# Moving one more batch's transposes of u from the DMA queue to TensorE, with newly searched instruction orders, in an attention and mixer kernel

## The chip, the cores and the metric

The kernel runs on one core of one Trainium2 chip. The metric is the device time in microseconds of one execution of the whole program. A ratio of two kernels is the mean time of one kernel's fast runs divided by the mean time of the other's fast runs of the same rounds, so it isn't quite the ratio of the medians that are quoted beside it. "Fast" leaves out executions more than 1.5% above the fastest of the same kernel; one run of the kernel before (300.56 us) fell out that way. Faster or slower needs 2%.

Engine names: PE is TensorE (matmul), PEld its weight loads, DVE is VectorE, ACT is ScalarE, POOL is GpSimd, SP is SyncE, which here only issues DMAs.

## The reference

Eight batches, each of 576 tokens. First comes attention with 8 heads of 64, an ALiBi bias and a causal window of 128; then a mixer on its result x (576 x 512 per batch).

```
scores = q @ k.T / 8 + slope[h] * -(distance), masked to 0 <= distance < 128
x      = softmax(scores) @ v                       # heads side by side: [576, 512]
u      = x + (relu(x.T @ w_tok1) @ w_tok2).T       # token mixing
out    = u + relu(u @ w_ch1) @ w_ch2               # channel mixing, 512 -> 1536 -> 512
```

## The kernel before: what the change and the argument touch

Every piece of work has a short name, and five hand-searched lists give the order in which the pieces are emitted. The order within the list is the order of instructions on every engine. One prime mark after a name means the next batch, two the one after it, and so on. The lists overlap batches: while batch b is in its channel mixing, batch b+1 has its attention and token mixing and batch b+2 its scores.

```python
U_DMA = (2, 3, 4, 5, 6, 7)      # batches whose u is transposed by DMA
DVE_RELU = (2, 3, 6)            # channel groups whose relu is on DVE, the others on ACT
PROLOGUE = """
J O q0 I q23 M0 FC l1 l23 W4 l0 qt G0 v2 q1 M1 v0 M3 cq0 M2 ck1 LC m1 ck0 v1 A0 cq1 A1 S00 ...
"""
SECOND = """ ... Lk''' C4 Lq''' v3''' v0''' v2''' ... U0' U2' UT' U3' U1'
S11'' X1' S00'' X0' X2' D20 D21 S21'' S10'' E0 D30 D22 E1 D31 P0'' D32 E2 X3'
"""
# ... FIRST, PERIOD (for batches 2 to 6) and LAST ...
```

The names that the text uses: q, l, qt, v load q, k, their tails and v (q0, q1, l0, l1 are plain fp32 loads on SP, which need the casts cq and ck; the rest are casting loads on POOL). J and I build the distance table and the identity matrix. A transposes q and k of batches 0 and 1 on TensorE, S makes a group of scores with its Exp (ACT) and mask multiplication (DVE), p/P is the product with v and its normalisation, k/K and u/U are the two halves of token mixing. G loads the three parts of w_ch1 (the tile WC1), H the halves of w_ch2. x/X transposes u, C is one of 12 channel groups of `u @ w_ch1` with its relu, D and E are the second channel product. T does the tail tokens of C. W is n matmuls on zeros that are only meant to keep TensorE's clock up. Lk, Lq, Zk, Zq load k and q of batches 2 to 7 and transpose them by DMA.

```python
def utrans(b, c):                                  # X
    def dma():
        nc.sync.dma_start_transpose(               # two 128-token chunks at a time
            out=utb[b % 2][:, c:c + 2]..., in_=ub[b % 2][:, c:c + 2, :]...)
    if b in U_DMA:
        return dma if c % 2 == 0 else lambda: None
    def f():
        t = M()[:, 0:256].bitcast(bf16)            # one of three PSUM banks of the mixer
        for cb in range(NCB):                      # 4 transposes by TensorE
            nc.tensor.transpose(t[:, cb * P:(cb + 1) * P],
                                ub[b % 2][:, c, cb * P:(cb + 1) * P], ident[:, :])
        cp = nc.vector.tensor_copy if c in X_DVE else nc.scalar.copy
        cp(out=utb[b % 2][:, c, :, :], in_=t...)
    return f

def ch1(b, ht):                                    # C: needs all four chunks of utb
    def f():
        t = M()
        for cb in range(NCB):
            nc.tensor.matmul(t[:, :], lhsT=WC1[:, cb, ht * P:(ht + 1) * P],
                             rhs=utb[b % 2][:, :, cb, :], start=..., stop=...)
        # ... relu on DVE or ACT
    return f

def score(b, kb, j):                               # S
    def f():
        s = S2()                                   # one of two score buffers, two banks each
        # ... matmuls into s, Exp on ACT from s to e, mask multiplication on DVE to p
    return f
```

The softmax here doesn't subtract the row's maximum and nothing guards it: scores larger than these inputs give would overflow.

## Time and profile before

| | before |
|---|---|
| time, median of 4 runs | 296.59 us (295.94 to 297.87) |
| span of the profiled run | 294.0 us |
| PE busy | 279.2 us, 95% |
| longest single wait of PE | 3.87 us, channel matmuls of batch 2 on the DMA transposes of u |

The page of the profile, parts 1 and 2: busy time of each engine, then 40 slices of the span (7.35 us each) with the busy share in tenths, the clock that TensorE was granted, and the busy share of the DMA engines.

```profile
PE 279.2 (95%) x2666; PEld 155.4 (53%) x2666; DVE 152.8 (52%) x302; ACT 135.3 (46%) x212; POOL 99.6 (34%) x128
...
PE   4889999999999869999999999999999999999995
...
PEclk9979999999999979999999999999999999999999
DMA  7999999899999999998999956995703320141013
```

PE is full except in the first slices, in slices 13 and 14 (counted from 0) and in the last. The clock has two dents, in slice 2 and slice 14. No other engine is close to full on average, so time can only come out of these few places. (The DMA engines are 90% busy or more in most of the first 23 slices.)

The waits of PE, from the same execution (who waited for what: total us, times, longest):

```profile
PE psM L471 <- DMA utb<-ub: 3.9, 1, 3.9
PE psM L227 <- ACT ks L729: 1.7, 1, 1.7
PE psM L227 <- DVE qs L729: 1.2, 1, 1.2
PE psM L227 <- DMA ks<-in_k_dram: 1.1, 2, 0.6
```

The first line is the wait in slices 13 and 14. L471 is the channel matmul, utb the transposed u. The others belong to the first microseconds. The view of windows gives the busy time of each engine in chosen stretches, then the granted clock, the share of the DMA engines (1 is one fully loaded set; over 1 means that the times of packets overlap) and GB/s:

```profile
core 0: us, PE busy (x) PEld busy (x) DVE busy (x) ACT busy (x) POOL busy (x), PEclk, DMA share, GB/s
13.00:17.00 4.00, 2.79 (x36) 1.49 (x33) 3.66 (x10) 4.00 (x7) 2.38 (x4) 1.00 2.25 163
17.00:20.60 3.60, 3.36 (x44) 2.81 (x45) 3.46 (x10) 0.99 (x3) 2.90 (x5) 0.53 1.35 199
93.00:97.00 4.00, 4.00 (x25) 1.73 (x24) 2.40 (x5) 3.31 (x4) 4.00 (x6) 1.00 2.11 185
101.00:105.40 4.40, 0.55 (x6) 0.27 (x5) 0.19 (x1) 0.58 (x1) 0.00 (x0) 1.00 1.77 152
106.00:109.00 3.00, 3.00 (x20) 1.46 (x18) 0.00 (x0) 1.06 (x2) 0.00 (x0) 0.50 1.61 253
```

Read it from the fourth row: PE is idle for most of 101 to 105.4 us. In the fifth row it is busy all the time, but at half the clock, so about half of the 3.4 us from 106 to 109.4 us is lost as well. In the third row, where the transposes were issued (93.1 us), the DMA share is 2.11. The second row shows another half-clock stretch in the prologue.

The timeline of the issuing queue and of PE shows both ends of the wait (start us, us, engine, line, what; in brackets the idle time before it and what ended it). The line between is from the view of DMA issues: the two transposes took 10.1 us from issue to landing as the median, and the later of them 10.9 us.

```profile
93.08 4.81 SPq L451 DMA_TRANSPOSE utb<-ub  x2
...
utb<-ub SPq DMA_TRANSPOSE x2, 10.1
...
105.41 3.08 PE L471 MATMUL psM<-utb,WC 128*128 128x512 bf16 x8 [3.87 <-DMA utb<-ub]
```

### The profile page before, as it was taken

How to read it: one execution, taken by the hardware profiler on the slowest of the kernel's cores; microseconds unless marked ns; L12 is line 12 of the kernel's file. 1: busy time of each engine (PE TensorE's matmuls, PEld its weight loads, DVE VectorE, ACT ScalarE, POOL GpSimd, SP SyncE). 2: the span in 40 equal slices, each digit the busy share in tenths (PEclk: the TensorE clock that was granted, in tenths of full speed). 3: DMA queues.
4: the chain of work that ended last, by engine and by line, in shares of the span. 5: the costliest groups of instructions: out<-in, count | busy, mean ns of one | idle time of the engine just before them, and what ended most of it. 6: DMA issues, size and time to landing. Idle time of an engine off the chain costs nothing.

```text
span 294.0 us, 6361 instructions
## 1 busy us (share of the span) xinstructions
PE 279.2 (95%) x2666; PEld 155.4 (53%) x2666; DVE 152.8 (52%) x302; ACT 135.3 (46%) x212; POOL 99.6 (34%) x128
## 2 busy tenths in 40 slices
PE   4889999999999869999999999999999999999995
PEld 2567546546564335654565455655565455645443
DVE  4587467557457406566467426555556626433012
ACT  6855896148525225425633554435542563203500
POOL 8786643098419501950079003930000000000000
PEclk9979999999999979999999999999999999999999
DMA  7999999899999999998999956995703320141013
GB/s 179 171 191 187 200 182 128 163 160 188 156 162 135 121 210 155 113 162 147 164 94 166 180 138 126 133 153 162 163 0 75 106 75 0 36 109 74 0 71 109
DMA packets 150748, 38.53 MB, mean 131 GB/s; under 512 B 137920, under 2 KB 146240, under 8 KB 150720
## 3 DMA queue, kind: packets, MB, share of 16 engines
q0 software_dynamic: 103152, 17.41, 78.1%
q1 hardware_dynamic: 47568, 20.72, 32.7%
q8 instruction: 21, 0.34, 0.5%
q14 instruction: 7, 0.06, 0.1%
HBM read 35.85 MB, written 9.44 MB: 154 GB/s over the span
## 4 chain that ended last, share of the span: by engine, by line
PE 83%; DMA 11%; DVE 2%; POOL 1%; ACT 1%; issue 0%; SPq 0%; POOLq 0%; ACTq 0%
PE psM L471 29%; PE psM L519 26%; DMA WC<-in_moe_w_ch_dram 5%; PE psM L429 4%; PE psM L404 4%; PE psT L486 4%; DMA utb<-ub 4%; PE psS L280 4%; PE psM L541 3%; PE psS L343 2%; DMA ks<-in_k_dram 2%; PE psS L339 2%; PE psS L371 1%; PE psM L500 1%; PE psS L284 1%; ACT pe L293 1%
## 5 line engine op out<-in xcount | busy, mean ns | idle before, releaser
L471 PE MATMUL psM<-utb,WC 128*128 128x512 bf16 x384 | 90.2, 383 | 3.9 <-DMA utb<-ub 3.9
L519 PE MATMUL psM<-WC,r 128*128 128x512 bf16 x372 | 87.0, 379 | 0.0
L293 ACT ACTIVATE pe<-psS 128x1024 bf16<-128x1024 f32 (+1 forms) x68 | 63.3, 987 | 38.0 <-PE psS L280 34.2
L477 ACT ACTIVATE r<-psM 128x512 bf16<-128x512 f32 x72 | 42.7, 607 | 55.3 <-PE psM L471 55.3
L471 PEld LDWEIGHTS <-WC 128*128 128x128 bf16 x384 | 35.5, 98 | 43.5 <-issue 6.1
L519 PEld LDWEIGHTS <-r 128*128 128x128 bf16 x372 | 34.2, 98 | 41.2 <-issue 3.8
L183 POOL DMA_DIRECT2D kn<-in_k_dram x24 | 21.1, 894 | 81.5 <-DMA kT<-kn 77.8
L299 DVE TENSOR_TENSOR pb<-pe,masks 128x1024 bf16<-128x1024 bf16 (+1 forms) x50 | 33.2, 670 | 27.4 <-ACT pe L293 27.3
L524 DVE TENSOR_TENSOR ob<-psM,ub 128x512 f32<-128x512 f32 x31 | 21.4, 689 | 24.8 <-PE psM L519 24.8
L183 POOL DMA_DIRECT2D vp<-in_v_dram x32 | 28.9, 953 | 2.3 <-DMA ks<-in_k_dram 1.6
L474 DVE TENSOR_SCALAR r<-psM 128x512 bf16<-128x512 f32 x24 | 16.6, 691 | 13.6 <-PE psM L471 12.7
L183 POOL DMA_DIRECT2D qn<-in_q_dram x24 | 21.3, 934 | 3.0 <-DMA WC<-in_moe_w_ch_dram 2.7
L303 DVE TENSOR_TENSOR pb<-pe,masks 128x512 bf16<-128x512 bf16 x16 | 6.8, 425 | 28.6 <-ACT pe L293 28.5
L431 DVE TENSOR_TENSOR ub<-psM,xb 128x512 bf16<-128x512 f32 x28 | 18.1, 686 | 5.4 <-PE psM L429 5.1
L353 DVE TENSOR_TENSOR xb<-psS,rt 128x512 bf16<-128x512 f32 x28 | 19.4, 692 | 1.0
L280 PE MATMUL psS<-qT,kT 64*128 64x256 bf16 x192 | 17.2, 280 | 1.2 <-ACT pe L293 0.7
L486 PEld LDWEIGHTS <-WC 128*128 128x128 bf16 x384 | 13.8, 100 | 3.9 <-issue 0.8
L429 PE MATMUL psM<-r,W 128*128 128x512 bf16 x56 | 15.4, 379 | 0.2 <-DVE ob L524 0.2
L343 PEld LDWEIGHTS <-pb 128*128 128x128 bf16 x224 | 13.3, 97 | 3.6 <-DVE pb L299 0.5
L343 PE MATMUL psS<-vp,pb 128*128 128x65 bf16 x224 | 15.1, 193 | 0.0
L486 PE MATMUL psT<-utt,WC 128*128 128x64 bf16 x384 | 14.3, 196 | 0.0
L489 ACT ACTIVATE r2t<-psT 128x384 bf16<-128x384 f32 x16 | 8.0, 498 | 11.8 <-PE psT L486 11.2
(119 smaller groups left out, 280.4 us busy)
## 6 DMA issues: line engine op xcount, KB each, us to landing
out_dram<-ob SPq DMA_DIRECT2D x31, 256.0 KB, 2.2
vp<-in_v_dram POOLq DMA_DIRECT2D x32, 128.0 KB, 6.6
kn<-in_k_dram POOLq DMA_DIRECT2D x24, 128.0 KB, 4.3
qn<-in_q_dram POOLq DMA_DIRECT2D x24, 128.0 KB, 5.1
WC<-in_moe_w_ch_dram POOLq DMA_DIRECT2D x3, 512.0 KB, 7.9
WC<-in_moe_w_ch_dram POOLq DMA_DIRECT2D x2, 768.0 KB, 12.3
out_dram<-ob SPq DMA_DIRECT2D x10, 128.0 KB, 2.3
qs<-in_q_dram POOLq DMA_DIRECT2D x3, 256.0 KB, 6.2
```

Of the source, the lines that this page charges most:

```text
L183: nc.gpsimd.dma_start(out=dst, in_=src[b, :, c * P:(c + 1) * P, :].rearrange("h s d -> s h d"))
L280: nc.tensor.matmul(s[:, h, a * 256:(a + 1) * 256], lhsT=kT[i][r, kb, hp, :], rhs=qT[i][r, kb:kb + 2, hp, :], start=True, stop=True)
L293: nc.scalar.activation(out=e[:, h, :], in_=s[:, h, :], func=ACT.Exp, scale=scale)
L299: nc.vector.tensor_tensor(out=p[:, :].rearrange("p (h x) -> p h x", h=2)[:, h], in0=e[:, h, :], in1=masks[:, j, h].rearrange("p h g a x -> ...
L343: nc.tensor.matmul(ov, lhsT=prob(b, qb, h, 0), rhs=vt[:, qb, h, 0:D + 1], start=first, stop=(hh == 3))
L353: nc.vector.tensor_tensor(out=xb[b % 2][:, qb, :].rearrange("p (b h d) -> p b h d", b=2, h=4), in0=ov[:, :, :, 0:D], in1=rv[:, :, :, None] ...
L429: nc.tensor.matmul(t[:, :], lhsT=W2[:, j, c * P:(c + 1) * P], rhs=r1[b % 2][:, j, :], start=(j == 0), stop=(j == 1))
L471: nc.tensor.matmul(t[:, :], lhsT=WC1[:, cb, ht * P:(ht + 1) * P], rhs=utb[b % 2][:, :, cb, :], start=(cb == 0), stop=(cb == NCB - 1))
L477: nc.scalar.activation(out=r2[b % 2][:, ht, :], in_=t[:, :], func=ACT.Relu)
L486: nc.tensor.matmul(o, lhsT=WC1[:, cb, ht * P:(ht + 1) * P], rhs=utt[(b // 2) % 2][:, cb, b % 2, :], start=(cb == 0), stop=(cb == NCB - 1))
L519: nc.tensor.matmul(t[:, :], lhsT=r2[b % 2][:, ht, c * P:(c + 1) * P], rhs=WC2[:, ht, :], start=(ht == 0), stop=(ht == NHT - 1))
L524: nc.vector.tensor_tensor(out=o[:, :], in0=t[:, :], in1=ub[b % 2][:, c, :], op=ALU.add)
```

## The change

The intent: TensorE transposes u of batches 0 to 2, DMA the others; some score groups of batch 0 in the banks of the mixer; all order lists searched anew. The diff, cut to its core:

```diff
-U_DMA = (2, 3, 4, 5, 6, 7)
-U_ACT = (1,)
-X_DVE = (1, 2, 3)
+U_DMA = (3, 4, 5, 6, 7)
+U_ACT = (0,)
+X_DVE = (1, 3)
 PROLOGUE = """
-J O q0 I q23 M0 FC l1 l23 W4 l0 qt G0 v2 q1 M1 v0 M3 cq0 M2 ck1 LC m1 ck0 v1 A0 cq1 A1 S00 v4 A2
-v3 S20 AT S10 A3 m0 LW S30 S01 q01' W1 G1 q23' S21 S11 l01' W1 p0 v3' l23' p1 k0 v1' S31 k1 u0
-u1 qt' p2 G2 H1 x1 p3 v0' k2 x0 u2 k3 A0' u3
+J M3 FC l23 M0 M1 W1 q0 q23 I l0 M2 cq0 W1 ck0 m0 l1 O q1 ck1 cq1 qt W3 v0 W4 A0 W3 v1 v2 s0 A1
+W2 S20 v3 t0 A2 AT v4 S10 LW A3 S30 m1 S01 l01' S11 q01' p0 G1 l23' p1 G0 W1 qt' e1 S31 k0 q23'
+S21 G2 H0 k1 v2' ek LC p2 A1' H1 A0' p3 u0 k2 u1 x0 v3' v4' k3 u2
 """
 # ... FIRST, SECOND, PERIOD and LAST in new orders as well ...
-SPLIT = (2, 3, 5, 7)
-x_DVE = (2, 3)
-k_DVE = (0, 1)
-AK_DVE = (5, 7)
-AQ_ACT = (4, 5, 6, 7)
-DVE_RELU = (2, 3, 6)
+SPLIT = (1, 2, 3, 4)
+S_M = (0, 5, 6, 7)
+x_DVE = (1, 2, 3)
+k_DVE = (0, 1, 3)
+AK_DVE = (2,)
+AQ_ACT = (0, 1, 4, 5, 7)
+DVE_RELU = (0, 2, 3, 4, 5, 7, 10, 11)
 # in score():
-            s = S2()
+            apart = b == 0 and j * 4 + kb in S_M
+            t2 = None if apart else S2()
+            s = [M(), M()] if apart else [t2[:, 0, :], t2[:, 1, :]]
 # new: score_half(kb, a), named s{kb} and t{kb}: one score group of batch 0 in two halves,
 # each as soon as its pair of heads is there
```

More of the change, by code (lines that the diff above doesn't have):

```diff
@@ L27 @@
+S21 G2 H0 k1 v2' ek LC p2 A1' H1 A0' p3 u0 k2 u1 x0 v3' v4' k3 u2
 """
 FIRST = """
-v4' UT x2 H0 A2' v2' Lk'' Lq'' x3 A3' C1 Zq'' AT' ek C6 e1 Zk'' A1' S11' S21' C4 Lk''' T0 v0''
-v1'' Lq''' v2'' C8 S01' S00' v4'' C9 C2 S10' C7 P0' v3'' ex C3 T1 S20' C0 S30' S31' v3''' C11 e2
-C5 v4''' P2' P3' v1''' v2''' C10 D00 P4' v0''' D01 P1' E0 D02 K0' K1' D10 D11 U1' D12 UT' X1'
-U2' U0' D20 D21 E1 D30 U3' E2 S11'' S00'' D31 D22 S10'' S20'' D32 S01'' T1' Zq''' X0'
+x1 v0' ex u3 A3' A2' AT' v1' Lk'' Lq'' UT x2 S00' S01' x3 Zq'' Zk'' T0 Lk''' S10' C8 v0'' v3''
@@ L33 @@
+C9 Lq''' S20' v0''' S21' v4'' C3 e2 C5 S31' S11' C0 C2 S30' C4 v2'' v4''' C7 P0' C11 P2' T1 C1
+C10 C6 E0 D00 P1' D01 P3' D02 v1'' v2''' P4' K0' K1' D10 E2 U1' D11 D12 Zq''' U2' v1''' UT' X1'
+U0' D30 D20 S20'' S11'' D21 D31 D32 Zk''' E1 D22 S01'' U3' S00'' X2'
 """
 SECOND = """
-X2 X3 S21' Zk'' S31' T0 C7 C5 P0' C8 C2 C6 P1' C11 C10 C3 S30' Lk''' C4 Lq''' v3''' v0''' v2'''
-C1 C0 C9 P3' P4' v1''' D00 P2' D01 D02 K0' K1' v4''' S20'' S01'' D10 D11 D12 U0' U2' UT' U3' U1'
-S11'' X1' S00'' X0' X2' D20 D21 S21'' S10'' E0 D30 D22 E1 D31 P0'' D32 E2 X3'
+X3 X0 T1 S30' S10' C3 C1 T0 C2 P0' C8 Lk''' C7 v3'' C5 S31' S21' C11 Lq''' v2''' C4 C10 C0 P4'
@@ L38 @@
+v0''' v4''' C9 C6 D00 P1' v3''' P3' D01 P2' D02 v1''' K0' K1' S01'' S20'' D10 D11 D12 U2' UT'
+U0' U3' S00'' U1' X0' S11'' X2' D20 D21 E0 S21'' S10'' D22 E1 X1' E2 P0'' D30 X3' D31 D32
 """
 PERIOD = """
-C11 C4 T0 S31' S30' C1 C5 C2 Zq'' C0 Zk'' C6 C9 P1' P4' C7 C3 C10 P3' Lk''' P2' C8 Lq''' v0'''
-K0' S01'' K1' S00'' v3''' v1''' D00 D01 D02 v2''' U0' T1 U1' U2' UT' U3' X1' D20 P0'' D10 X2'
-v4''' D21 S21'' S11'' X3' X0' D22 D30 D11 D12 S10'' S20'' D31 D32 E0 E1 E2
+C7 T0 C4 C3 C0 S31' S30' Zq'' C8 C2 Zk'' C11 C9 P1' C1 C10 P2' P3' Lk''' C6 C5 Lq''' P4' v0'''
@@ L43 @@
+K0' K1' S01'' S00'' D00 v2''' v1''' D01 D02 T1 U2' U1' UT' U0' v3''' U3' D20 X2' X3' X1' D21
+P0'' D10 D11 v4''' S11'' S10'' X0' D12 D30 D22 D31 S20'' S21'' E0 E1 D32 E2
 """
 LAST = """
-C6 C1 C3 C7 C11 T1 C2 C9 C8 T0 C0 C5 C10 C4 D00 D01 D02 D20 D10 E0 D21 D22 E1 E2 D11 D12 D30 D31
+C7 T1 C0 C1 C2 C9 C6 C8 C10 C11 C4 C3 T0 C5 D00 E0 D01 D10 D02 E1 D11 D20 D21 D22 E2 D12 D30 D31
 D32
@@ L260, with score_half, f, g @@
     probs = {}
+    half = {}
+    def score_half(kb, a):
+        def f():
+            if a == 0:
+                n = qrot[0]
+                qrot[0] += 1
+                half[kb] = (S2(), pe[n % len(pe)], pb[n % len(pb)])
+                probs[0, kb, 0] = half[kb][2]
+            s, e, p = half[kb]
+            cs = slice(a * 256, (a + 1) * 256)
+            for h in range(2):
+                r = slice(h * D, (h + 1) * D)
+                nc.tensor.matmul(s[:, h, cs], lhsT=kT[0][r, kb, a, :],
+                                 rhs=qT[0][r, kb:kb + 2, a, :], start=True, stop=True)
+            nc.scalar.activation(out=e[:, :, cs], in_=s[:, :, cs], func=ACT.Exp, scale=scale)
+            def g():
+                nc.vector.tensor_tensor(
+                    out=p[:, :].rearrange("p (h x) -> p h x", h=2)[:, :, cs], in0=e[:, :, cs],
+                    in1=masks[:, 0, :, a].rearrange("p h g x -> p h (g x)"), op=ALU.mult)
+            later(MASK_LATER, g)
+        return f
     tok1_banks = {}
@@ L279, in f @@
                     for h, r in enumerate(halves):
-                        nc.tensor.matmul(s[:, h, a * 256:(a + 1) * 256], lhsT=kT[i][r, kb, hp, :],
+                        nc.tensor.matmul(s[h][:, a * 256:(a + 1) * 256], lhsT=kT[i][r, kb, hp, :],
                                          rhs=qT[i][r, kb:kb + 2, hp, :], start=True, stop=True)
@@ L283, in f @@
                 for h, r in enumerate(halves):
-                    nc.tensor.matmul(s[:, h, a * P:(a + 1) * P], lhsT=kT[i][r, kb, hp, :],
+                    nc.tensor.matmul(s[h][:, a * P:(a + 1) * P], lhsT=kT[i][r, kb, hp, :],
                                      rhs=qT[i][r, kb, hp, :], start=True, stop=True)
@@ L288, in f @@
                         c = 256 + t * P + a * ST
-                        nc.tensor.matmul(s[:, h, c:c + ST], lhsT=kT[i][r, kb + t, hp, :],
+                        nc.tensor.matmul(s[h][:, c:c + ST], lhsT=kT[i][r, kb + t, hp, :],
                                          rhs=qT[i][r, NC, hp, 0:ST], start=True, stop=True)
-            parts = (slice(0, 1), slice(1, 2)) if b == 0 and j * 4 + kb in SPLIT else (slice(0, 2),)
-            for h in parts:
-                nc.scalar.activation(out=e[:, h, :], in_=s[:, h, :], func=ACT.Exp, scale=scale)
+            split = apart or b == 0 and j * 4 + kb in SPLIT
+            parts = (slice(0, 1), slice(1, 2)) if split else (slice(0, 2),)
+            for n, h in enumerate(parts):
+                nc.scalar.activation(out=e[:, h, :], in_=s[n][:, None, :] if split else t2[:, :, :],
+                                     func=ACT.Exp, scale=scale)
             probs[b, kb, j] = p
@@ L797, in names @@
             d["O"] = lambda: ones_v(0)
+            for kb in range(NC - 1):
+                d[f"s{kb}"], d[f"t{kb}"] = score_half(kb, 0), score_half(kb, 1)
             for j in range(2):
```

## The prediction

> **What bounds the kernel now.** TensorE. Part 1 of the page gives PE 279.2 of 294.0 us busy (95%), DVE 52%, ACT 46%. In windows of 7 us, PE has almost no gap from 35 to 98 us, nor from 110 us to the end. So time can be won from PE's idle 14.8 us, from stretches at a lowered clock, and from PE's work. By the PE timeline and the granted clock in windows of 1 us:
> - One wait of 3.87 us (101.5 to 105.4 us): the first channel matmuls of batch 2 wait for the DMA transposes of u, the largest entry of the waits on PE. They took 10.9 us to land, against 3.2 to 7.5 us in later batches; the DMA share is 2.1 to 2.4 then.
> - After it the clock is 0.50 from 106 to 109.4 us: about 1.8 us lost. The Trainium skill, "TensorE: Matmul & The Clock Gate", Part 1, says that an idle window halves the clock and about 3.4 us of activity restores it; the trace agrees (matmuls 427 ns apart, then 216).
> - Prologue up to 31 us: 6.8 us idle in small waits; clock 0.5 from 17.2 to 20.6 us (about 1.7 us lost).
> - The end, about 3.5 us.
>
> **What the change removes.** Batch 2's u goes through 16 TensorE transposes and four evictions, as batch 1's does. That removes the wait and the halved clock: -5.7 us. It adds about +1.0 us on PE (12 such transposes of batch 1 took 0.73 us); the evictions (0.42 us DVE, 0.62 us ACT) lie on engines with slack. Net -4.7 us, all on the critical path.
>
> **What it moves in the prologue.** Three score groups use the mixer's banks, one is halved, so fewer scores wait for psS; WC1 is loaded after W1 and W2; 9 warming matmuls instead of 4 come first, 6 later instead of 2. Exp on ACT is serial (about 1 us per group, eight groups) and starts about 1.5 us earlier (before: 9.0 us). But the first channel group now is C8, which needs the last third of WC1; that landed at 32.5 us, and I estimate 31 us now. Before it the new order does about 2.6 us of PE work that the old did after its first channel group (31.2 us). By durations PE gets there at about 32.3 us: a gain of 1 to 2.
>
> **Steady state.** Same work. Eight of twelve relus on DVE instead of three: DVE about 60%, no effect. Batches 3 to 7 keep DMA transposes, with slack of only 1.2 to 2.5 us in batches 3 to 5; a new wait in one of them is the likeliest loss. I allow 0.6 us.
>
> **Sum.** -4.7 - 1.6 + 0.6 = -5.7 us: 296.5 becomes 290.8 us, range 288.3 to 294.0. The 2% line is at 290.6: faster by over 2% 0.48, within 2% 0.49, slower 0.03.
>
> **What would show it.** Waits on PE: the entry "DMA utb" gone or below 1 us. Granted clock 1.0 all through batch 2. PE busy about 280 us in a span of about 288. Batch 2's transposes of u take 0.9 to 1.1 us. Channel matmuls without gaps from 31 to 33 us on. Early transposes at full clock, and no longer half-clock stretch in the prologue than before.
>
> **What would make it wrong.** C8 waiting for WC1 beyond 33 us, or a long cold stretch in the prologue: no gain there, 292 to 293 us. DMA transposes of batch 3 or 5 late, with a halved clock after: +2 to 4 us. PE waiting for PSUM banks behind the reordered evictions. In the other direction, a prologue shortened by the full 2 to 3 us: 288.5 to 289.5 us.

## The result, and the profile after

The changed kernel took 292.33 us (median of 4 runs, 291.4 to 292.6) against 296.59 us; the ratio is 0.9846, with a 95% interval of 0.9806 to 0.9885. That is within the 2% line and inside the predicted range, 1.5 us above the predicted value.

The same lines of the page as before:

```profile
PE 278.1 (96%) x2691; PEld 154.0 (53%) x2691; DVE 178.3 (61%) x349; ACT 114.6 (39%) x177; POOL 99.7 (34%) x128
...
PE   7769799999999999999999999999999999999995
...
PEclk9799999999999999999999999999999999999999
DMA  6999999899999996996999968994803320042014
```

The hole and the dent in slices 13 and 14 are gone. The first slices are no better than before: PE has 7, 7, 6, 9, 7 where it had 4, 8, 8, 9, 9, and part of that busy time is the added warming matmuls. The waits of PE:

```profile
PE psS L276 <- DVE qT L233: 2.8, 1, 2.8
PE psM L228 <- DMA qs<-in_q_dram: 1.5, 1, 1.5
PE psM L640 <- DVE rtt L625: 1.1, 1, 1.1
...
PE psS L307 <- DVE qT L233: 0.8, 1, 0.8
PE psM L640 <- DVE r L646: 0.8, 1, 0.8
```

No line names utb any more, and every line belongs to the prologue. In windows (columns as above):

```profile
5.70:9.30 3.60, 0.83 (x7) 0.30 (x4) 0.81 (x3) 1.16 (x3) 3.60 (x5) 1.00 1.24 163
10.90:14.20 3.30, 3.30 (x41) 2.00 (x41) 2.33 (x6) 2.52 (x6) 2.96 (x5) 0.50 2.35 158
14.90:22.00 7.10, 4.26 (x80) 3.01 (x74) 6.74 (x22) 6.43 (x13) 6.03 (x9) 1.00 1.34 197
...
101.00:105.00 4.00, 4.00 (x33) 2.23 (x32) 2.25 (x6) 0.58 (x1) 1.25 (x2) 1.00 2.18 197
```

The last row is the stage that was idle before: PE is full, at full clock, while the DMA share is still 2.18. The first row is a new hole, from 5.7 to 9.3 us; the second a half-clock stretch of the same length as the old one; the third shows DVE 95% and ACT 91% busy while PE is at 60%.

The timeline of DVE and PE tells what the new hole is, and where the prologue ends:

```profile
8.49 0.43 DVE L758 CAST qs<-qf 128x512 bf16<-128x512 f32 x1 [2.95 <-DMA qf<-in_q_dram]
8.83 0.75 DVE L233 COPY qT<-psM 128x256 bf16<-128x256 bf16 x2
9.30 0.29 PE L276 MATMUL psS<-qT,kT 64*128 64x256 bf16 x2 [2.77 <-DVE qT L233]
...
30.83 0.41 PE L228 MATMUL psM<-ident,qs 128*64 128x128 bf16 x8 [1.47 <-DMA qs<-in_q_dram]
...
35.19 1.91 PE L500 MATMUL psM<-utb,WC 128*128 128x512 bf16 x8
```

The second head pair of q landed only at about 8.5 us (6.5 us before). In the new list its cast (cq1) stands ahead of A0, so on DVE it stands in front of the eviction of the first pair's transposes, whose input had been ready since about 5.1 us. The first full channel group starts at 35.19 us.

A tally of the two profiled executions. An estimate: at 31.2 us the old kernel started its first channel group, and the new order does about 2.6 us of PE work before its own first one that the old did later; so the old kernel had come equally far at about 33.8 us, the new one at 35.2 us. In these two executions the prologue then cost about 1.4 us more. In batch 2 the wait (3.87 us) and the half clock (about 1.8 us) are gone and 16 transposes are added (the four groups of four took 1.06 us in the timeline): -4.6 us. Together -3.2 us, and the spans differ by 294.0 - 290.9 = 3.1 us. The medians differ by 4.3 us: the profiled execution of the kernel before (295.74 us) was a quick one, that of the changed kernel (292.60 us) the slowest of its four, so the loss of 1.4 us is not that of a typical pair.

What the half clock alone is worth can't be told from whole runs. In the rounds of the experiments below, five of the 32 fast runs of the kernel before had a mean clock of 0.998 or more, so hardly any half-clock stretch, and took 295.8 us on average; the 17 with 0.985 to 0.990, which fits two stretches, took 296.6 us. The two stretches together lose about 3.5 us of TensorE's time by durations, but the runs differ by 0.8 us. The 1.8 us in the tally is therefore a reading of one execution.

### The profile page after: what moved, and what is told of

It reads as the page before. It is cut to its first block, busy times and chain, and to the rows that moved or that the text cites. A ratio compares the mean times of both kernels' runs of the same rounds, so it can differ in the third digit from the quotient of the medians.

```text
span 290.9 us, 6418 instructions
## 1 busy us (share of the span) xinstructions
PE 278.1 (96%) x2691; PEld 154.0 (53%) x2691; DVE 178.3 (61%) x349; ACT 114.6 (39%) x177; POOL 99.7 (34%) x128
## 4 chain that ended last, share of the span: by engine, by line
PE 87%; DMA 9%; POOL 1%; issue 1%; DVE 1%; SPq 0%; ACT 0%
PE psM L500 28%; PE psM L548 27%; PE psM L458 4%; PE psS L307 4%; DMA qs<-in_q_dram 4%; PE psT L515 4%; PE psM L570 4%; PE psM L433 4%; DMA kT<-kn 3%; DMA qf<-in_q_dram 2%; PE psS L372 2%; PE psS L368 1%; PE psS L400 1%; PE psM L529 1%; PE psS L311 1%; PE psM L228 1%
## 5 line engine op out<-in xcount | busy, mean ns | idle before, releaser
L321 ACT ACTIVATE pe<-psS 128x1024 bf16<-128x1024 f32 (+1 forms) x64 | 58.9, 973 | 48.8 <-PE psS L307 34.9
L500 PEld LDWEIGHTS <-WC 128*128 128x128 bf16 x384 | 35.1, 98 | 38.6 <-issue 1.1
L503 DVE TENSOR_SCALAR r<-psM 128x512 bf16<-128x512 f32 x64 | 43.3, 687 | 19.8 <-PE psM L500 19.8
L328 DVE TENSOR_TENSOR pb<-pe,masks 128x1024 bf16<-128x1024 bf16 (+1 forms) x52 | 33.0, 639 | 31.1 <-ACT pe L321 30.8
L506 ACT ACTIVATE r<-psM 128x512 bf16<-128x512 f32 x32 | 19.1, 602 | 30.3 <-PE psM L500 30.3
L518 ACT ACTIVATE r2t<-psT 128x384 bf16<-128x384 f32 x16 | 7.9, 494 | 32.3 <-PE psT L515 32.2
L307 PE MATMUL psS<-qT,kT 64*128 64x256 bf16 x180 | 15.3, 276 | 1.1 <-DVE qT L233 0.8
L372 PE MATMUL psS<-vp,pb 128*128 128x65 bf16 x224 | 15.1, 193 | 0.0
L458 PE MATMUL psM<-r,W 128*128 128x512 bf16 x56 | 14.9, 380 | 0.0
L515 PEld LDWEIGHTS <-WC 128*128 128x128 bf16 x384 | 13.2, 98 | 3.1
L451 ACT ACTIVATE r<-psM 128x512 bf16<-128x512 f32 x7 | 4.2, 597 | 25.2 <-PE psM L442 25.2
```

The lines of the kernel that those rows point to most:

```text
L307: nc.tensor.matmul(s[h][:, a * 256:(a + 1) * 256], lhsT=kT[i][r, kb, hp, :], rhs=qT[i][r, kb:kb + 2, hp, :], start=True, stop=True)
L321: nc.scalar.activation(out=e[:, h, :], in_=s[n][:, None, :] if split else t2[:, :, :], func=ACT.Exp, scale=scale)
L328: nc.vector.tensor_tensor(out=p[:, :].rearrange("p (h x) -> p h x", h=2)[:, h], in0=e[:, h, :], in1=masks[:, j, h].rearrange("p h g a x -> ...
L372: nc.tensor.matmul(ov, lhsT=prob(b, qb, h, 0), rhs=vt[:, qb, h, 0:D + 1], start=first, stop=(hh == 3))
L458: nc.tensor.matmul(t[:, :], lhsT=W2[:, j, c * P:(c + 1) * P], rhs=r1[b % 2][:, j, :], start=(j == 0), stop=(j == 1))
L503: nc.vector.tensor_scalar(out=r2[b % 2][:, ht, :], in0=t[:, :], scalar1=0.0, scalar2=None, op0=ALU.max)
```

## The experiments

All were timed in turn with the kernel before on the same chip. The changed kernel itself was run again with the first three.

> The changed kernel once more, as the yardstick for the other three on this chip. All theories expect a ratio to the kernel before of 0.983 to 0.987 (about 292 us).

It gave 292.31 us and a ratio of 0.9858 (0.9826 to 0.9891). Its fast runs have a mean of 292.22 us, those of the kernel before 296.38 us.

### 1. Batch 2's transposes back to DMA, in the changed kernel

```diff
-U_DMA = (3, 4, 5, 6, 7)
+U_DMA = (2, 3, 4, 5, 6, 7)
```

> The changed kernel with batch 2's u back on DMA transposes, all else as changed. Theory 1 (nearly all of the gain is the removed wait and the half-clock stretch after it; the new order lists win nothing net): about 4.7 us slower than the changed kernel, 296 to 297.5 us, and the waits on PE show the DMA transposes of u again with 3 to 5 us. Theory 2 (the newly searched orders would hide the DMA transposes as well, and the gain is the orders'): within 1 us of the changed kernel and no such wait.

It gave 296.69 us, ratio 1.0008 (0.9972 to 1.0044). The means of the fast runs are 296.65 us against 292.22 us of the changed kernel on the same chip: 4.4 us. The wait is back as the first line of the waits of PE:

```profile
PE psM L500 <- DMA utb<-ub: 3.3, 1, 3.3
PE psS L276 <- DVE qT L233: 2.2, 1, 2.2
```

and the clock was 0.50 again from 107 to 110 us. Theory 1 holds and theory 2 falls. The profiled execution also had two half-clock stretches in the prologue, where that of the changed kernel had one; but the mean clock over six runs is nearly the same (0.987 and 0.989), so that can hardly be what makes the 4.4 us. This run also says that everything else in the change, taken together and with these transposes on DMA, is worth nothing that can be measured (+0.1%, with an interval of 0.4% on either side).

### 2. Only the transposes, in the kernel before

```diff
-U_DMA = (2, 3, 4, 5, 6, 7)
+U_DMA = (3, 4, 5, 6, 7)
```

> The kernel before with only batch 2's u moved to TensorE transposes, old order lists. Theory 1: the whole gain or more, ratio to the kernel before 0.983 to 0.986 (291.6 to 292.4 us), with the wait of 3.87 us and the 0.50 clock at 106 to 109 us gone. Theory 2: the old lists have no good place for these transposes, new waits on PSUM banks eat half of it or more, 294 us or above.

It gave 293.06 us, ratio 0.9889 (0.9857 to 0.9921): 3.3 us of gain from one constant. That lies between the two expectations. Two waits show why it isn't the whole:

```profile
PE psM L461 <- DVE ub L431: 0.8, 1, 0.8
PE psM L471 <- DVE utb L464: 0.5, 1, 0.5
```

The old list had these names placed for DMA: the transposes come directly after u is evicted, and the last one directly before the channel group that needs it, which costs 0.8 + 0.5 = 1.3 us. The new lists spread the four groups from 94 to 102.5 us and have neither wait. So the new orders can contribute this much; against this run the whole change is 0.9 us ahead, with intervals that overlap.

The comparison isn't quite like for like, and it settles something about the prologue. The clock was full from start to end in all six runs (0.999 to 1.0), also in the prologue, whose list this edit leaves alone:

```profile
17.00:20.60 3.60, 2.48 (x55) 1.95 (x53) 3.27 (x10) 1.18 (x3) 2.82 (x4) 1.00 1.35 199
```

Yet in its profiled execution the first channel group started at 31.89 us, not earlier than the 31.20 us of the kernel before with its half clock there. So the half clock in the prologue isn't what held up its end. Why it is missing here is open.

### 3. Why the DMA transposes were late: loads taken away

Two runs of the kernel before with loads left out of the second list. Both compute something else, since batch 4 then reuses older tokens.

```diff
 SECOND = """
-... S30' Lk''' C4 Lq''' v3''' v0''' ...
+... S30' Lk''' C4 v3''' v0''' ...             # before_nolq
+... S30' C4 ...                               # before_noload: no Lk''', Lq''', v0''' to v4''' at all
```

> The kernel before without batch 4's load of q in the second list (wrong result on purpose: batch 4's q transpose reads batch 3's tokens). Theory 1b (batch 2's DMA transposes of u landed after 10.9 us because the loads for batch 4 were in flight with them): they land in 5 to 7 us, the 3.87 us wait is gone or below 0.5 us, and the run is 4 to 5.5 us faster than the kernel before. Rival (the transposes are slow because two of them follow one another on one queue, whatever else is loaded): still 9 to 11 us and a wait of 3 us or more.

The landing became 9.4 us (10.9 before), the wait 2.3 us, the time 293.94 us (2 runs, ratio 0.9917). Neither expectation was met. (The result still passed the comparison with the reference, so a check of the output alone wouldn't have shown that batch 4's q was wrong.) Hence the second run:

> The kernel before without any of batch 4's loads of k, q and v in the second list (wrong result on purpose: batch 4 reuses older tokens). Taking only q away moved the landing from 10.9 to 9.4 us and the wait from 3.9 to 2.3 us, which neither theory had. Theory 1b (loads in flight delay the DMA transposes): without any, they land in 3.1 to 4 us, as those of the last two batches do, with no wait and no half clock; about 5 us faster than the kernel before (ratio 0.980 to 0.985). Rival (something else in that stage, such as the late eviction of u or the issue from one queue): still 8 us or more and a wait of 1 us or more.

The two transposes landed after 3.3 and 4.8 us, no wait on utb is left, and the time is 290.26 us (2 runs, ratio 0.9794 with an interval of 0.9725 to 0.9862, so against the 2% line the verdict is unclear). The output is wrong (relative error 0.45). The median landing of the two, then in windows the stage that had the hole:

```profile
utb<-ub SPq DMA_TRANSPOSE x2, 4.1
...
93.00:97.00 4.00, 4.00 (x25) 1.78 (x24) 2.44 (x4) 3.62 (x4) 0.00 (x0) 1.00 0.63 118
...
101.00:105.00 4.00, 4.00 (x64) 2.57 (x63) 0.50 (x1) 2.46 (x5) 0.00 (x0) 1.00 0.48 131
```

The DMA share is 0.63 instead of 2.11 and PE stays full. So it was the loads of batch 4 as a whole that held the transposes up, and q's part of them was about a quarter. The Trainium skill, "DMA: Bandwidth & Descriptors", Queues, rings and completion order, says that each DMA engine goes round between the queues that have work, packet by packet; a transpose on one queue sharing with a full queue of loads fits that, though no run here shows the turns themselves.

### 4. The prologue: one wait at a time

Three single edits of the changed kernel's first list, each aimed at one wait of its profile.

```diff
-J M3 FC l23 M0 M1 W1 q0 q23 I l0 ...                    # after_ident
+J I M3 FC l23 M0 M1 W1 q0 q23 l0 ...
-... O q1 ck1 cq1 qt W3 v0 W4 A0 W3 v1 v2 s0 A1          # after_a0
+... O q1 qt W3 v0 W4 A0 W3 v1 v2 s0 ck1 cq1 A1
-... q01' p0 G1 l23' p1 G0 W1 qt' e1 S31 k0 q23'         # after_load
+... q01' p0 l23' q23' G1 p1 G0 W1 qt' e1 S31 k0
```

> The changed kernel with the identity built on GpSimd before the first casting loads of k and q instead of after them, as the old list had it. The casting loads then start about 0.5 us later. Theory 3 (in the changed kernel they crowd the plain loads of the second head pair of k and q, which land at 6.9 and 8.5 us against 5.8 and 6.5 us before; the DVE cast that waits for q holds up the eviction queued behind it): second q lands at about 6.5 us, the PE wait of 2.77 us before the first half score group falls below 1 us, and the half-clock stretch at 11 to 14 us moves or shrinks. In time 0 to 2 us faster: TensorE then still waits for the batch 1 q load that lands at 30.8 us, so I expect only about 0.3 us (291.9). A rival (the prologue is one chain and every us at its start counts): 1.5 to 2.5 us faster.

292.26 us, ratio 0.9866 (0.9832 to 0.99), beside 0.9858 for the changed kernel on the same chip: no difference. The second part of k came earlier, as expected (cast at 5.70 us, 6.95 before), but the second part of q didn't (cast at 8.14 us). Half of theory 3 falls: a later start of the casting loads doesn't bring q back to 6.5 us. What does delay it is open.

> The changed kernel with the casts of the second head pair of k and q queued after the transposes of the first pair and their evictions, instead of before them. Theory 3b (the wait of 2.0 to 2.8 us before the first half score group is a queue effect: the DVE cast that waits for q stands ahead of an eviction whose input is long ready): the first half score group starts before 7.5 us instead of at 9.0 to 9.3 us. TensorE then waits for q at the next transposes instead, so I expect the time to change by less than 0.5 us. Rival (it is one chain): 1.5 us faster or more.

291.81 us, ratio 0.9845 (0.9821 to 0.987). The wait before the first half group is gone, and stands before the next transposes instead, a little longer:

```profile
9.81 0.41 PE L228 MATMUL psM<-ident,qs 128*64 128x128 bf16 x8 [3.07 <-DVE qs L758]
```

So the blocked eviction in the DVE queue was real, but it hid behind the arrival of q; freeing it moved the wait by one step.

> The changed kernel with batch 1's second load of q issued before the first two parts of WC1 instead of between them and the third. Theory 4 (what holds the end of the prologue is the arrival of batch 1's q, 30.8 us, and that alone): the wait of 0.6 to 1.5 us on DMA qs is gone and the kernel is 0.5 to 1.5 us faster than the changed one (ratio 0.981 to 0.985). Rival (the loads only change places; then WC1 or the compute chain holds TensorE as long): same time within 0.3 us, a wait of about the same size elsewhere before 35 us.

292.23 us, ratio 0.9853 (0.9826 to 0.9879). The wait on q at 30.8 us is gone, as meant, and the time didn't follow. Its windows show where it went in the profiled execution:

```profile
9.00:15.00 6.00, 5.57 (x58) 3.09 (x58) 3.73 (x10) 3.52 (x8) 5.28 (x8) 0.50 2.14 164
...
22.80:26.00 3.20, 3.20 (x48) 3.00 (x49) 2.86 (x10) 1.13 (x3) 1.70 (x2) 0.51 1.26 207
```

TensorE ran two long stretches at half clock here, where the first profile of the changed kernel had one of 3.3 us. The first of them begins at about 9 us, ahead of anything that the edit moves, so the edit isn't what put it there: the changed kernel itself, profiled again as after_again, was at half clock from about 8.2 to 15.1 us. This run therefore doesn't say cleanly what the earlier load is worth.

### 5. All of them together

The edits after_a0 and after_load, seven more warming matmuls ahead of A1, and in the list FIRST C8 and C9 exchanged with C6 and C1, so that the first channel groups don't need the last part of WC1.

```diff
-... q1 ck1 cq1 qt W3 v0 W4 A0 W3 v1 v2 s0 A1
+... q1 qt W3 v0 W4 A0 W3 v1 v2 s0 ck1 cq1 W4 W3 A1
-... T0 Lk''' S10' C8 v0'' v3'' C9 ... T1 C1 C10 C6 E0 ...
+... T0 Lk''' S10' C6 v0'' v3'' C1 ... T1 C9 C10 C8 E0 ...
 # and the edit of after_load
```

> A try at a version that beats both: the two edits above, seven more warming matmuls between the first half group and the second pair's transposes so that the clock isn't halved at 11 to 14 us, and ch1 groups 6 and 1 in the first list exchanged with 8 and 9, so that the first channel groups need only the first two parts of WC1. If the prologue's losses (idle about 8 us, half clock about 1.6 us) can be had back: 289.5 to 291 us. If they only move to the next wait: 292 us as the changed kernel.

291.09 us, correct, ratio 0.9823 (0.9798 to 0.9849); six runs from 290.85 to 291.85 us. It is the fastest correct kernel. Against the kernel before, the verdict is unclear, as the interval lies on both sides of 2%. Its lead over the others is small: on the same chip after_a0 has 291.83 and this has 291.16 us as mean (0.2%), with five of its six runs below all five of after_a0. No wait of 1 us is left in its prologue apart from the very first. The half clock is still there in the profiled run (0.51 from 15.5 to 18.5 us), though two of the six runs had a mean clock of 1.0 and were no faster (291.12 and 290.85 us). To remove it, a further version put the identity first and three warming matmuls before the group S01:

```diff
-J M3 FC l23 M0 M1 W1 q0 q23 I l0 ...  S30 m1 S01
+J I M3 FC l23 M0 M1 W1 q0 q23 l0 ...  S30 m1 W3 S01
```

> The faster version once more, with the identity built first and three warming matmuls in the wait of 0.8 us ahead of the group S01, to keep the clock full at 15 to 18.5 us. If that half clock costs: 0.5 to 1 us faster than the version before it (ratio 0.979 to 0.981, 290.2 to 290.6 us). If TensorE only waits for DVE there anyway (it is busy over 90%): the same, ratio 0.981 to 0.984.

291.75 us, ratio 0.9842 (0.9802 to 0.9883), on another chip. The clock was full in the profiled run (0.999 to 1.0 in five of the six runs, 0.994 in the other), and the time is no better. Waits of TensorE on DVE and on a load of v stand in its profile instead:

```profile
PE psM L640 <- DVE rtt L625: 1.2, 1, 1.2
PE psS L372 <- DMA vp<-in_v_dram: 1.1, 1, 1.1
```

### 6. The other two parts of the change undone

```diff
-S_M = (0, 5, 6, 7)                            # after_nobank
+S_M = ()
-DVE_RELU = (0, 2, 3, 4, 5, 7, 10, 11)         # after_relu
+DVE_RELU = (2, 3, 6)
```

> The changed kernel with all score groups of batch 0 in the two score buffers again (no group in the mixer's banks). Theory 5 (the banks matter in the prologue: the scores of the second half must otherwise wait for Exp to free a buffer): new waits of TensorE on Exp or on the normalisation of 1 us or more between 15 and 24 us, and 0.5 to 1.5 us slower than the changed kernel. Rival (ACT and DVE, busy over 90% from 15 to 23 us, hold the prologue, and a bank more doesn't make them faster): within 0.4 us of the changed kernel.

292.77 us, ratio 0.9884 (0.984 to 0.9928). New waits appear, and the two of 1.1 and 0.8 us on token mixing (L640) are gone:

```profile
PE psS L601 <- DVE pb L328: 1.0, 1, 1.0
...
PE psS L601 <- DMA W<-in_moe_w_tok_dram: 0.8, 1, 0.8
PE psS L307 <- ACT pe L278: 0.7, 1, 0.7
...
PE psS L311 <- DVE xt L626: 0.4, 1, 0.4
```

The third and fourth are waits for a score buffer that Exp or the normalisation has to free, as theory 5 said. But the third (0.7 us) stands in the profiles of after_dma2 and after_best as well, which have the banks, so only the fourth (0.4 us) can be put down to this edit; and the new waits replace others. The difference from the changed kernel (0.9846 and 0.9858 on other chips) is within the intervals, so a gain from the banks isn't shown.

> The changed kernel with three relus of the channel groups on DVE as before, nine on ACT. Both theories on record (no effect, because neither engine is the bottleneck after 35 us) expect within 0.4 us of the changed kernel. If the searched order relies on the split, waits of PE on Exp or relu appear in the first list and it is 1 us slower or more.

292.61 us, ratio 0.9873 (0.9833 to 0.9913): not different from the changed kernel, with no new wait after 35 us. ACT was busy 137.0 us instead of 114.6, DVE 153.2 instead of 178.3.

## Why the prediction was right, and where its sum was off

- **The bottleneck and the wait in batch 2: right.** "The entry 'DMA utb' gone": it is. "Granted clock 1.0 all through batch 2": it is. "0.9 to 1.1 us" for the transposes: 1.06 us. The net of -4.7 us was measured as 4.4 us by putting the DMA transposes back. Shown, by undoing it in one kernel and doing it alone in the other.
- **The cause of the late landing, only hinted at in the prediction by the DMA share: right, and now shown** by taking the loads away (10.9 to at most 4.8 us).
- **"A gain of 1 to 2" us in the prologue: wrong, and this is the term that was mis-sized.** The new lists with DMA transposes are no faster than the old lists (ratio 1.0008), and in the two profiled runs the prologue was about 1.4 us longer. The prediction let Exp start "about 1.5 us earlier" and TensorE reach the first channel group at about 32.3 us; Exp started at 9.62 us (9.03 before) and the group at 35.19 us. It says nothing of when the second pair of q lands (6.5 us in the old profile) or what the changed order does to it; it landed at about 8.5 us, and the DVE cast in front of A0's eviction passed the delay on. That this one wait cost the gain isn't shown: with the cast moved (after_a0) the wait moved one step and the gain was not measurable, and with the waits of 1 us and more in the prologue removed (after_best) about 1 us came back (means of 291.16 and 292.22 us, on different chips).
- **The last part of WC1 at about 31 us: wrong.** It was issued at 20.14 us and took 13.2 us, so it landed at 33.3 us (and in the old trace at 33.6 us, not at 32.5). It had no effect, as TensorE was later still.
- **The 0.6 us allowed for new waits in batches 3 to 7: not needed.** No wait on utb appears there; the transposes landed within 7.7 us.
- **"No effect" of the relus on DVE: right**, by after_relu; DVE rose to 61%.

Of the other signs that the prediction named, PE was busy 278.1 us in a span of 290.9 (280 in 288 expected), and the channel matmuls ran without gaps from 35.2 us on (31 to 33 expected). The prologue's half clock lasted 3.3 us in the first profile, no longer than before, but 6.8 us in the second (after_again).

The value came within 1.5 us because the main effect held; that the allowance (0.6 us) covered part of the missing prologue gain (1.6 us) was luck. The time measured, 292.3 us, is the one that the prediction gave for no gain in the prologue (292 to 293 us), though it expected C8's wait for WC1 or a long cold stretch as the reason.

What stays open: what delays the second pair of q, how the lost prologue gain divides among its waits, and what decides where the half-clock stretches of the prologue fall.

## What to carry to other kernels

Where one engine is full, look for the one long wait, and count what follows it too: here, in the profiled execution, the slow clock after a wait of 3.87 us cost almost half as much again, and a transpose of 1 us on the busiest engine was cheaper than a free one that came late. When order lists are searched anew, a landing time from the old profile isn't an input for the new one, and an instruction that waits for a load should stand behind those in its queue whose inputs are ready (here that moved a wait without a measurable gain). In a start-up phase where two engines are over 90% busy and loads are saturated, removing one wait mostly shows the next.

## What the Trainium skill lacked or had wrong

- "TensorE: Matmul & The Clock Gate", HAM oscillation, gives the rule that TensorE must have no idle gaps over about 3.4 us. It isn't enough here: in the kernel before, TensorE was busy 2.79 of the 4.00 us from 13 to 17 us, its longest single wait there was 0.52 us, and from 17.2 to 20.6 us the clock was at half. The page's second failure mode (micro-idles between groups) is the nearer one, but gives no threshold. In before_pe2, with the same list for this stretch, TensorE was busy 3.08 of the same 4.00 us and the clock stayed full. The other way round, 4.26 busy us of 7.10 from 14.9 to 22 us brought no half clock in the changed kernel.
- The same page, Part 1, says that the window of about 3.4 us runs freely, so that the point at which the clock rises in a warm-up varies by about 0.5 us. The runs agree with 3.4 us as a usual length, but the place varies by more: in two executions of the changed kernel the slow stretch began at 10.9 us and lasted 3.3 us, or began at 8.2 us and lasted 6.8 us. The page doesn't say when it is one window and when two.
- "DMA: Bandwidth & Descriptors", DMA Transpose, gives no latency of a transpose under load. Here one pair of SBUF transposes (128 x 1024 elements each) landed after 3.3 and 4.8 us with a DMA share of 0.63, and after up to 10.9 us with a share of 2.11.
- No page gives a figure for the latency of a plain load on SP beside casting loads on POOL. The same fp32 load of 256 KB landed after 4.2 us in the kernel before and after 6.1 us in the changed one.
